# A combiner-attention and GeGLU kernel: keys kept as overlapping slices with the block maxima inside, values cast in the load, block means in column groups, and a new step order

## The chip, the cores and the metric

The kernel runs on one core of a Trainium2 chip. The metric is the device time of one execution in microseconds (us); "before" is 333.6 us (median of 3 runs, 333.51 to 334.36). Engines are named as in the profile: PE is TensorE, PEld its weight loads, DVE VectorE, ACT ScalarE, POOL GpSimd, SP SyncE. Transfers that change the type (fp32 in memory, bf16 on chip) are issued from POOL's queue; plain ones from the queues of SP and ACT. All executions used below were in the fast state (none lay more than 1.5% above the fastest of its kernel); medians are quoted.

## The reference, cut to what matters

```python
# attention: 4 batches, 8 heads, 768 positions, head size 64
k_sum = k.reshape(B, H, 24, 32, D).max(axis=3)       # maximum of each block of 32 keys
v_sum = v.reshape(B, H, 24, 32, D).mean(axis=3)      # mean of each block of 32 values
scores_l = scale * q @ k.T,   kept where |i - j| < 16          # the band
scores_s = scale * q @ k_sum.T + log(32)                       # 24 block scores
a = softmax(concat(scores_l, scores_s));  x = a @ concat(v, v_sum)
# GeGLU with a gated residual, 3072 tokens, 512 -> 1536 -> 512
out = x + sigmoid(x @ w_res) * ((gelu(x @ w_gate) * (x @ w_val)) @ w_out)
```

## The kernel before

The work is cut into 8 units u: half of a batch (384 positions). Each unit has a front part A of 12 FFN steps `fo` (gate and value products, Gelu, product `gvT`) and a back part B with the residual gate r, the down projection f and the output. The attention of unit u+1 is woven into part B of unit u; the loads, turns (transposes on PE) and block means of the next batch are woven into part A. In the profile tp are turns of K or Q, s the scores, P their exponentials under the mask, ao the attention output, xp its turns and xT their copy, g and vv the gate and value products, vs the block means, and th and o the last two operations of a unit's output.

In the attention, 64 queries of a head meet a window of 96 keys. The 128 rows of a score tile hold 96 band scores and, in rows 96 to 127, the block scores. Two products make them: one against a 128-wide slice of the turned keys, whose last 32 rows are garbage, then one that overwrites those rows:

```python
def k_step(b, hp, ...):                      # turn K of one head pair, then the block maxima
    transpose_pair(k_sb[b], kT[b % 2][hp], WIN, hp, pool, tag, copy)
    nc.vector.tensor_reduce(out=ksum[b % 2][hp][:, 0:NB], in_=kT..., op=ALU.max)

def s_step(u, hp, st):
    for t in range(HT):
        for hh in range(2):
            nc.tensor.matmul(s[:, hh, t*QT:(t+1)*QT], kt[ps, tt*QT:tt*QT+128], qt[...])
    for hh in range(2):
        nc.tensor.matmul(s[96:128, hh, 0:TU], ksum[b % 2][hp][ps, :], qt[...])   # block scores
    ...                                      # exp on ACT, mask product on DVE

def vsum_mm(b, pool, tag):                   # block means: 12 products into the same 32 rows
    for t in range(NT):
        nc.tensor.matmul(vs[96:128, :], bmat[:, t, :], vext[b % 2][0:BAND, t, :, 0:D], ...)
    nc.vector.tensor_copy(vsum[b % 2][96:128, :], vs[96:128, :])
# vsum_bc: the means are then copied by POOL behind each of the 12 value windows of vext
```

V of batch 0 comes as fp32 through the SP and ACT queues into a stage `vst` and is cast by 12 copies. K turns of the next batch stand in even units (after fo 1, 4, 7, 10), Q turns and the block means (after fo 6) in odd ones. [...]

The softmax here doesn't subtract the row's maximum and nothing guards it: scores larger than these inputs give would overflow.

Of the kernel before, what the change touches and what calls it, by code (L numbers as in the profile page):

```python
# [15 lines left out]
def kernel(  # L16
# [30 lines left out]
    KPAD = 832  # L47
# [6 lines left out]
    stage = ctx.enter_context(tc.tile_pool(name="stage", bufs=1))  # L54
# [12 lines left out]
    kT = [[const.tile([128, KPAD], BF16, name=f"kT{i}_{p}") for p in range(NP)] for i in range(2)]  # L67
    qT = [[const.tile([128, S], BF16, name=f"qT{i}_{p}") for p in range(NP)] for i in range(2)]
    ksum = [[const.tile([128, 32], BF16, name=f"ks{i}_{p}") for p in range(NP)] for i in range(2)]
    vext = [const.tile([128, NT, H, D + 1], BF16, name=f"vext{i}") for i in range(2)]  # L70
    vsum = [const.tile([128, DM], BF16, name=f"vsum{i}") for i in range(2)]
    w_gate = wpool.tile([128, KO, DFF], BF16, name="w_gate")
# [3 lines left out]
    vst = stage.tile([BAND, NT, H, D], F32, name="vst")  # L76
# [16 lines left out]

    k_sb, q_sb = {}, {}

    with tc.manual_schedule():

        k_sb[0] = load_qk(k, 0, 2, "k_sb")
        q_sb[0] = load_qk(q, 0, 2, "q_sb")
        nc.vector.memset(vst[0:32, 0], 0.0)  # L100
        nc.vector.memset(vst[64:96, NT - 1], 0.0)
        for t in range(NT):
            r0, r1, src = v_window(0, t)
            eng = nc.sync if t % 2 == 0 else nc.scalar
            eng.dma_start(out=vst[r0:r1, t], in_=src)  # L105


        nc.vector.memset(ident[:], 0.0)
        nc.gpsimd.affine_select(out=ident[:], in_=ident[:], compare_op=ALU.not_equal, fill=1.0,
                                base=0, pattern=[[-1, 128]], channel_multiplier=1)  # L110
        for i in range(2):
            for p in range(NP):
                nc.vector.memset(kT[i][p][:, 0:WIN], 0.0)
                nc.vector.memset(kT[i][p][:, WIN + S:KPAD], 0.0)
                nc.vector.memset(ksum[i][p][:], 0.0)
# [3 lines left out]
        nc.vector.memset(bmat[:], 1.0 / BLK)  # L119
        for i in range(2):  # L120
            nc.vector.memset(vext[i][:, :, :, D:D + 1], 1.0)
            nc.vector.memset(vext[i][0:32, 0, :, 0:D], 0.0)
            nc.vector.memset(vext[i][64:96, NT - 1, :, 0:D], 0.0)
        nc.gpsimd.affine_select(out=bias_t[96:128, :], in_=bias_t[96:128, :], compare_op=ALU.is_ge,
# [7 lines left out]
        nc.gpsimd.affine_select(out=bmat[:], in_=bmat[:], compare_op=ALU.is_ge, fill=0.0,  # L132
                                base=-WIN, pattern=[[QT, NT], [-BLK, 32]], channel_multiplier=1)
        nc.gpsimd.affine_select(out=bmat[:], in_=bmat[:], compare_op=ALU.is_ge, fill=0.0,
                                base=BLK - 1 + WIN, pattern=[[-QT, NT], [BLK, 32]], channel_multiplier=-1)
        nc.gpsimd.affine_select(out=bmat[:], in_=bmat[:], compare_op=ALU.is_ge, fill=0.0,
                                base=-WIN, pattern=[[0, NT], [0, 32]], channel_multiplier=1)
        nc.gpsimd.affine_select(out=bmat[:], in_=bmat[:], compare_op=ALU.is_ge, fill=0.0,
                                base=WIN + QT - 1, pattern=[[0, NT], [0, 32]], channel_multiplier=-1)
# [23 lines left out]
        def transpose_pair(src, dst, pad, hp, pool, tag, copy):  # L163
            tp = pool.tile([128, PJ, PP], BF16, tag=tag, name="tp")
            for j in range(PJ):
                for hh in range(2):
                    nc.tensor.transpose(tp[hh * 64:hh * 64 + 64, j, :], src[:, 2 * hp + hh, j, :],  # L167
                                        ident[0:PP, 0:PP])
            o = dst[:, pad:pad + S].rearrange("d (p j) -> d p j", j=PJ)
            t_in = tp.rearrange("d j p -> d p j")  # L170
            if copy == "act":
                nc.scalar.copy(o, t_in)
            else:
                nc.vector.tensor_copy(o, t_in)

        def k_step(b, hp, pool, tag, copy="act"):
            transpose_pair(k_sb[b], kT[b % 2][hp], WIN, hp, pool, tag, copy)
            nc.vector.tensor_reduce(
                out=ksum[b % 2][hp][:, 0:NB],
                in_=kT[b % 2][hp][:, WIN:WIN + S].rearrange("d (n w) -> d n w", w=BLK),  # L180
                axis=mybir.AxisListType.X, op=ALU.max)

        def q_step(b, hp, pool, tag, copy="act"):
            transpose_pair(q_sb[b], qT[b % 2][hp], 0, hp, pool, tag, copy)
# [7 lines left out]

        def vsum_bc(b, lo, hi, eng):
            src = vsum[b % 2][96:128, :].rearrange("p (h d) -> p h d", d=D)
            src = src.unsqueeze(1).to_broadcast([32, hi - lo, H, D])
            eng.tensor_copy(vext[b % 2][96:128, lo:hi, :, 0:D], src)  # L196

        def s_step(u, hp, st):
            b, half = u // 2, u % 2
            s = ps_s.tile([128, 2, 512], F32, tag="s", name="s")  # L200
            kt, qt = kT[b % 2][hp], qT[b % 2][hp]
            for t in range(HT):
                tt = half * HT + t
                for hh in range(2):
                    ps = slice(hh * 64, hh * 64 + 64)
                    nc.tensor.matmul(s[:, hh, t * QT:(t + 1) * QT], kt[ps, tt * QT:tt * QT + 128],  # L206
                                     qt[ps, tt * QT:(tt + 1) * QT], start=True, stop=True,
                                     skip_group_check=True)
            for hh in range(2):
                ps = slice(hh * 64, hh * 64 + 64)  # L210
                nc.tensor.matmul(s[96:128, hh, 0:TU], ksum[b % 2][hp][ps, :],  # L211
                                 qt[ps, half * TU:(half + 1) * TU], start=True, stop=True,
                                 skip_group_check=True)
# [23 lines left out]
        def xt_step(u, g, st, pool, tag):  # L237
            xp = pool.tile([128, 2, TU], BF16, tag=tag, name="xp")
            for i in range(2):
                ko = 2 * g + i  # L240
                for sub in range(NSUB):
                    nc.tensor.transpose(xp[:, i, sub * 128:(sub + 1) * 128],
                                        st["xn"][:, sub, ko * 128:(ko + 1) * 128], ident[:])
            nc.vector.tensor_copy(st["xT"][:, 2 * g:2 * g + 2, :], xp[:])  # L244
# [20 lines left out]
        def out_step(u, st, gvT, sub, part):  # L265
            ss = slice(sub * 128, (sub + 1) * 128)
            if part == 0:
                r = ps_mm.tile([128, 512], F32, tag="mm", name="r")
                for ko in range(KO):
                    nc.tensor.matmul(r[:], st["xT"][:, ko, ss], w_res[:, ko, :],  # L270
                                     start=(ko == 0), stop=(ko == KO - 1))
                th = work.tile([128, DM], F32, tag="th", name="th")
                nc.scalar.activation(th[:], r[:], AF.Tanh, scale=0.5)  # L273
                f = ps_mm.tile([128, 512], F32, tag="mm", name="f")
                for fo in range(4):
                    nc.tensor.matmul(f[:], gvT[:, fo, ss], w_out[:, fo, :],  # L276
                                     start=(fo == 0), stop=False)
                st["f"], st["th"] = f, th
            else:
                f, th = st["f"], st["th"]  # L280
                for fo in range(4, FO):
                    nc.tensor.matmul(f[:], gvT[:, fo, ss], w_out[:, fo, :],  # L282
                                     start=False, stop=(fo == FO - 1))
                nc.vector.scalar_tensor_tensor(th[:], th[:], 1.0, f[:], ALU.add, ALU.mult)  # L284
                o = work.tile([128, DM], F32, tag="o", name="o")
                nc.vector.scalar_tensor_tensor(o[:], th[:], 0.5, st["xn"][:, sub, :], ALU.mult, ALU.add)  # L286
                row = u * TU + sub * 128
                nc.sync.dma_start(out=out[row:row + 128, :], in_=o[:])

        def v_loads(b):  # L290
            for t in range(NT):
                r0, r1, src = v_window(b, t)
                nc.gpsimd.dma_start(out=vext[b % 2][r0:r1, t, :, 0:D], in_=src)  # L293


        for hp in range(NP):
            k_step(0, hp, ps_mm, "mm", "act")
            q_step(0, hp, ps_mm, "mm", "vec" if hp % 2 else "act")
        for t in range(NT):
            if t % 3 == 2:  # L300
                nc.scalar.copy(vext[0][0:BAND, t, :, 0:D], vst[:, t])
            else:
                nc.vector.tensor_copy(vext[0][0:BAND, t, :, 0:D], vst[:, t])
        st = new_unit()
        s_step(0, 0, st)
        s_step(0, 1, st)
        vsum_mm(0, ps_t, "t")
# [7 lines left out]
        xt_step(0, 0, st, ps_mm, "mm")  # L315
# [76 lines left out]
```

## Time and profile before

| stretch, before | us | how to read it |
|---|---|---|
| start to the first r of unit 0 | 71.8 | start of the first r product in the timeline |
| first r of unit u to first r of unit u+1 | 37.4, 34.6, 37.4, 34.6, 37.4, 32.3, 31.7 | part B of u and part A of u+1 |
| last first r to the end of the span | 15.2 | part B of unit 7 |

An interval from r to r is named here by its two units: 0 to 1, 2 to 3 and 4 to 5 hold the block means and Q turns; 1 to 2 and 3 to 4 hold K turns; the last two hold neither. The interval 6 to 7 also lacks the first score step of a next unit (21 instructions on ACT against 22 in 5 to 6, 249 products on PE against 263), which is why it is the shortest.

The list of waits of TensorE before (engine, tile and line, what it waited for: us in total, number of waits, longest):

```profile
PE tp L167 <- DMA k_sb<-in_k_dram: 13.9, 2, 9.3
PE g L255 <- DVE xT L244: 9.7, 7, 1.4
```

The timeline of the start before (start, us, engine, line, operation, output and inputs, shapes; in brackets the idle time in front and what ended it):

```profile
30.64 5.30 PE L189 MATMUL vs<-vext_113,bmat 96*32 96x512 bf16 x12
...
30.93 0.42 DVE L303 CAST vext_113<-vst 96x512 bf16<-96x512 f32 x1 [5.35 <-DMA vst<-in_v_dram]
...
46.45 1.38 PE L255 MATMUL g<-xT,w_gate 128*128 128x384 bf16 x4
...
54.41 0.85 PE L167 MATMUL tp<-ident,k_sb 96*64 96x96 bf16 x16 [4.64 <-DMA k_sb<-in_k_dram]
```

The fp32 V is complete only near 31 us, the block-mean product follows, and when the FFN has begun it stops: the K turns of batch 1 stand in unit 0's part A and wait 4.6 us for a load that has only come at 54.4 us.

Three intervals, r to r, in the windows view (busy us of each engine with the number of instructions, granted clock, DMA share, GB/s):

```profile
core 0: us, PE busy (x) PEld busy (x) DVE busy (x) ACT busy (x) POOL busy (x), PEclk, DMA share, GB/s
71.84:109.27 37.43, 35.99 (x339) 18.98 (x337) 17.53 (x34) 16.76 (x26) 7.43 (x6) 1.00 0.07 24
109.27:143.84 34.57, 33.14 (x327) 17.96 (x325) 19.92 (x37) 16.75 (x26) 8.71 (x12) 1.00 1.34 102
285.54:317.20 31.66, 30.23 (x249) 16.47 (x248) 16.22 (x32) 13.12 (x21) 0.00 (x0) 1.00 0.07 26
```

PE is busy about 96% of each, so from 72 us on only what shortens PE's own work, or removes PE's few waits, counts. The one regular wait is at the start of each unit:

```profile
158.03 0.50 PE L242 MATMUL xp<-ident,xn 128*128 128x128 bf16 x6
158.30 0.69 DVE L284 SCALAR_TENSOR_TENSOR th<-th,f 128x512 f32<-128x512 f32 x1 [0.91 <-PE f L282]
...
159.02 0.69 DVE L286 SCALAR_TENSOR_TENSOR o<-th,xn 128x512 f32<-128x512 f32 x1
159.63 0.55 DVE L244 COPY xT<-xp 128x768 bf16<-128x768 bf16 x1
160.23 0.48 PE L255 MATMUL g<-xT,w_gate 128*128 128x384 bf16 x2 [1.38 <-DVE xT L244]
```

The last turns of the attention output (xp) are on PE at 158.0, but their copy xT stands on DVE behind th and o of the old unit, and g waits 1.38 us for it.

### The profile page before, as it was taken

How to read it: one execution, taken by the hardware profiler on the slowest of the kernel's cores; microseconds unless marked ns; L12 is line 12 of the kernel's file. 1: busy time of each engine (PE TensorE's matmuls, PEld its weight loads, DVE VectorE, ACT ScalarE, POOL GpSimd, SP SyncE). 2: the span in 40 equal slices, each digit the busy share in tenths (PEclk: the TensorE clock that was granted, in tenths of full speed). 3: DMA queues.
4: the chain of work that ended last, by engine and by line, in shares of the span. 5: the costliest groups of instructions: out<-in, count | busy, mean ns of one | idle time of the engine just before them, and what ended most of it. 6: DMA issues, size and time to landing. Idle time of an engine off the chain costs nothing.

```text
span 332.4 us, 6258 instructions
## 1 busy us (share of the span) xinstructions
PE 284.7 (86%) x2640; PEld 153.8 (46%) x2640; DVE 162.4 (49%) x324; ACT 134.8 (41%) x202; POOL 71.1 (21%) x88
## 2 busy tenths in 40 slices
PE   0254574999899998999899989998999989998994
PEld 0241242554455445544445445544555446444641
DVE  5172651557533465556433665557333754474423
ACT  0343311464344543564336335553535523552320
POOL 7614741400007740000009440000042000000000
PEclk9999997999999999999999999999999999999999
DMA  8999999900100999001002997001000100010001
GB/s 155 206 197 192 202 207 178 92 3 35 65 0 3 159 154 113 1 2 63 34 0 26 198 151 52 1 34 40 26 2 0 65 34 0 2 63 34 0 33 63
DMA packets 54843, 23.95 MB, mean 72 GB/s; under 512 B 37408, under 2 KB 51744, under 8 KB 54816
## 3 DMA queue, kind: packets, MB, share of 16 engines
q0 software_dynamic: 42208, 14.98, 55.6%
q1 hardware_dynamic: 8032, 7.44, 8.0%
q10 hardware_dynamic: 4576, 1.15, 1.6%
q8 instruction: 20, 0.33, 0.4%
q14 instruction: 7, 0.06, 0.1%
HBM read 32.24 MB, written 6.29 MB: 116 GB/s over the span
## 4 chain that ended last, share of the span: by engine, by line
PE 75%; DMA 10%; DVE 9%; SPq 2%; issue 1%; POOL 1%; ACT 0%; DVEq 0%; ACTq 0%
PE g L255 19%; PE vv L259 19%; PE f L282 13%; DMA vst<-in_v_dram 6%; PE r L270 5%; PE f L276 5%; DMA k_sb<-in_k_dram 4%; PE vs L189 4%; PE tp L167 3%; DVE th L284 3%; DVE o L286 3%; PE ao L229 2%; PE s L206 2%; SPq L105 2%; PE s L211 2%
## 5 line engine op out<-in xcount | busy, mean ns | idle before, releaser
L255 PE MATMUL g<-xT,w_gate 128*128 128x384 bf16 x384 | 80.8, 330 | 9.7 <-DVE xT L244 9.7
L263 DVE TENSOR_TENSOR gvT<-ge,vv 128x384 bf16<-128x384 f32 x96 | 53.1, 553 | 73.2 <-PE vv L259 73.2
L262 ACT ACTIVATE ge<-g 128x384 f32<-128x384 f32 x96 | 47.1, 491 | 96.2 <-PE g L255 63.0
L259 PE MATMUL vv<-xT,w_val 128*128 128x384 bf16 x384 | 78.8, 328 | 0.0
L255 PEld LDWEIGHTS <-w_gate 128*128 128x128 bf16 x384 | 35.4, 99 | 34.9 <-issue 13.8
L259 PEld LDWEIGHTS <-w_val 128*128 128x128 bf16 x384 | 37.8, 98 | 25.5 <-issue 0.8
L215 ACT ACTIVATE P<-s,bias_t 128x768 bf16<-128x768 f32 x32 | 28.8, 901 | 46.0 <-PE s L211 45.9
L282 PE MATMUL f<-w_out,gvT 128*128 128x512 bf16 x192 | 45.4, 379 | 0.0
L196 POOL COPY vext_114<-vsum_116 32x2048 bf16<-32x2048 bf16 x6 | 11.1, 1893 | 86.7 <-DVE vsum_116 L191 86.7
L284 DVE SCALAR_TENSOR_TENSOR th<-th,f 128x512 f32<-128x512 f32 x24 | 16.5, 688 | 26.7 <-PE f L282 26.7
L282 PEld LDWEIGHTS <-gvT 128*128 128x128 bf16 x192 | 17.9, 98 | 20.6 <-issue 1.2
L218 DVE TENSOR_TENSOR P<-P,maskt 128x768 bf16<-128x768 bf16 x32 | 20.0, 626 | 14.5 <-ACT P L215 14.4
L270 PE MATMUL r<-w_res,xT 128*128 128x512 bf16 x96 | 24.9, 381 | 0.0
L276 PE MATMUL f<-w_out,gvT 128*128 128x512 bf16 x96 | 24.6, 379 | 0.0
L293 POOL DMA_DIRECT2D vext_114<-in_v_dram x24 | 18.2, 761 | 20.1 <-DMA q_sb<-in_q_dram 5.6
L167 PE MATMUL tp<-ident,k_sb 96*64 96x96 bf16 x256 | 10.1, 232 | 13.9 <-DMA k_sb<-in_k_dram 13.9
L196 POOL COPY vext_113<-vsum_115 32x2048 bf16<-32x2048 bf16 (+1 forms) x4 | 9.1, 2303 | 50.1 <-DVE vsum_115 L191 50.1
L235 DVE TENSOR_TENSOR xn<-ao,rz 128x384 bf16<-128x384 f32 x32 | 17.8, 558 | 1.1
L229 PEld LDWEIGHTS <-P 128*64 128x64 bf16 x384 | 9.2, 115 | 19.3 <-DVE P L218 10.1
L273 ACT ACTIVATE th<-r 128x512 f32<-128x512 f32 x24 | 14.3, 595 | 7.6 <-PE r L270 6.7
L286 DVE SCALAR_TENSOR_TENSOR o<-th,xn 128x512 f32<-128x512 f32 x24 | 16.6, 692 | 0.8
L167 PEld LDWEIGHTS <-k_sb 96*64 96x64 bf16 x256 | 7.9, 127 | 17.8 <-DMA k_sb<-in_k_dram 14.3
(139 smaller groups left out, 239.4 us busy)
## 6 DMA issues: line engine op xcount, KB each, us to landing
out_dram<-o SPq DMA_DIRECT2D x24, 256.0 KB, 2.0
k_sb<-in_k_dram POOLq DMA_DIRECT2D x3, 768.0 KB, 7.7
q_sb<-in_q_dram POOLq DMA_DIRECT2D x3, 768.0 KB, 11.3
vext_114<-in_v_dram POOLq DMA_DIRECT2D x20, 96.0 KB, 11.5
w_gate<-in_moe_w_gate_dram POOLq DMA_DIRECT2D x6, 256.0 KB, 16.1
w_val<-in_moe_w_val_dram POOLq DMA_DIRECT2D x6, 256.0 KB, 16.0
w_out<-in_moe_w_out_dram POOLq DMA_DIRECT2D x3, 512.0 KB, 14.0
vst<-in_v_dram ACTq DMA_DIRECT2D x5, 192.0 KB, 11.4
```

The lines of the kernel that those rows point to most:

```text
L167: nc.tensor.transpose(tp[hh * 64:hh * 64 + 64, j, :], src[:, 2 * hp + hh, j, :], ident[0:PP, 0:PP])
L196: eng.tensor_copy(vext[b % 2][96:128, lo:hi, :, 0:D], src)
L215: nc.scalar.activation(P.rearrange("p a t q -> p a (t q)"), s[:, :, 0:TU], AF.Exp, scale=scale, bias=bias_t[:])
L255: nc.tensor.matmul(g[:, 0:TU], w_gate[:, ko, fs], st["xT"][:, ko, :], start=(ko == 0), stop=(ko == KO - 1))
L259: nc.tensor.matmul(vv[:, 0:TU], w_val[:, ko, fs], st["xT"][:, ko, :], start=(ko == 0), stop=(ko == KO - 1))
L262: nc.scalar.activation(ge[:], g[:, 0:TU], AF.Gelu)
L263: nc.vector.tensor_mul(gvT[:, fo, :], ge[:], vv[:, 0:TU])
L270: nc.tensor.matmul(r[:], st["xT"][:, ko, ss], w_res[:, ko, :], start=(ko == 0), stop=(ko == KO - 1))
L276: nc.tensor.matmul(f[:], gvT[:, fo, ss], w_out[:, fo, :], start=(fo == 0), stop=False)
L282: nc.tensor.matmul(f[:], gvT[:, fo, ss], w_out[:, fo, :], start=False, stop=(fo == FO - 1))
L284: nc.vector.scalar_tensor_tensor(th[:], th[:], 1.0, f[:], ALU.add, ALU.mult)
L286: nc.vector.scalar_tensor_tensor(o[:], th[:], 0.5, st["xn"][:, sub, :], ALU.mult, ALU.add)
```

## The change

The intent: get rid of the second score product by writing the keys as 12 slices of 128 columns per head pair, 96 keys of a window with overlap plus 24 block maxima (copied into every slice); cast V of batch 0 in its load, as the other batches; run the block-mean products of batches 1 to 3 in four column groups of 32, side by side; warm PE up with 16 dummy products; put K turns, Q turns and block means one after another into odd units; copy xT in quarters instead of halves. The core of the diff:

```diff
-    kT = [[const.tile([128, KPAD], ...)]]; ksum = [[const.tile([128, 32], ...)]]
+    kW = [[const.tile([128, NT, 128], BF16, ...) for p in range(NP)] for i in range(2)]
-    vst = stage.tile([BAND, NT, H, D], F32, name="vst")          # and its 12 loads and 12 casts
+        v_loads(0)                                               # POOL queue, casts in the load
+            nc.vector.memset(vext[i][96:128, :, :, 0:D], 0.0)    # for i in 0, 1: before k_sb is loaded
@@ k_step
+            nc.scalar.copy(kw[:, 1:NT - 1, 0:BAND]..., src)      # 10 overlapping windows: 960 columns
+            nc.vector.tensor_copy(kw[:, 0, WIN:BAND]..., ...)    # the two edge windows
+            nc.vector.tensor_copy(kw[:, NT - 1, 0:BAND - WIN]..., ...)
+            nc.vector.tensor_reduce(out=ks..., op=ALU.max)
+            nc.vector.tensor_copy(kw[:, :, BAND:BAND + NB], ks.unsqueeze(1).to_broadcast([128, NT, NB]))
@@ s_step
-                nc.tensor.matmul(s[96:128, hh, 0:TU], ksum[b % 2][hp][ps, :], ...)
@@ block means of batches 1 to 3
+            for i in range(3):
+                for g in range(4):
+                    nc.tensor.matmul(vs[32 * g:32 * g + 32, :], bgrp[:, i, :], vext[...][0:BAND, 3 * g + i, :, 0:D],
+                                     ..., tile_position=(0, 32 * g))
+            nc.vector.tensor_copy(vpart[:], vs[:])
+            for g in range(4):
+                nc.sync.dma_start(out=vsum[b % 2][96 + 6 * g:102 + 6 * g, :], in_=vpart[32 * g:32 * g + 6, :])
@@ start
+        for i in range(16):
+            nc.tensor.matmul(wp[:], warm[:, 0:128], warm[:], start=True, stop=True)
@@ part A of odd units
+                    if fo < NP:          k_step(nb, fo, ps_t, "t")
+                    elif fo < 2 * NP:    q_step(nb, fo - NP, ps_t, "t")
+                    elif fo == 2 * NP:   vsum_grp(nb, ps_t, "t"); vsum_bc(nb, ...) x3 on POOL
@@ end of part B
+            end_step(u, st, 2)           # th, o
+            if nst:
+                xt_step(n, 2, nst, ps_t, "t"); xt_step(n, 3, nst, ps_mm, "mm")
 [...]
```

## The prediction

> **What bounds the kernel now.** (1) Start: in the timeline the first FFN matmul runs at 46.4 us, then TensorE stands from 49.8 to 54.4 us, because the K turns of batch 1 wait for their load (list of waits: tp on k_sb, 13.9 us in 2, the first 9.3). Before that the chain of waits runs through the fp32 V staging load (last casts at 27.8 and 30.9 us), the block-mean product (5.3 us) and the serial attention of unit 0. The r product of unit 0 stands at 71.9 us. (2) From there TensorE runs back to back (windows: busy about 96%): 245.5 us for seven units, then a 15 us tail. A plain unit takes 31.8-32.3 us, one with K turns 34.6, one with Q turns and block means 37.4.
>
> **Removed.** Block-score products: 0.27 us per head pair, 1.08 per unit. Part sits where VectorE sets the pace (th 0.70, o 0.69, reciprocal and xn 0.68, mask 0.5 between two f products), so I count 0.8: -5.6 us over seven units. Block means: 12 products of 512 columns, 2.73 us, become four 32-column groups side by side (Trainium skill, "TensorEngine Tiling (Array Packing)", When to Use Tiling; here 16 turns of 96 columns in 0.46 us already overlap): estimate 0.9 us, -5.5 us over three. The V stage and its 12 casts go. The K load of batch 1 is needed a unit later: the 4.6 us stall goes.
>
> **Added.** K copy of 960 instead of 768 elements on ACT (0.80 -> estimate 0.96 us); on VectorE two edge copies and a broadcast (estimate 0.6 us) per K step. K steps fall on four successive FFN steps: VectorE needs about 2.1 us per 1.86 us of PE, +0.8 us per odd unit. The block means go through four SyncE DMAs (0.33 us issue, 2 us landing) before three POOL copies of 1.9 us, with about 7.7 us until the values are wanted. These copies fall on the mask product and o; one mask took 2.9 instead of 0.56 us beside a POOL copy at 38 us (Trainium skill, "SBUF — State Buffer", Who interferes with whom: such a pair shares a locked port). I charge +2 us per odd unit. Otherwise the step order is nearly the old one: the 1.4 us wait of g for xT at a unit's start (9.7 us in all) stays, since o still precedes the last xT copies.
>
> **Start after.** Two memsets of 6144 elements (estimate 5.2 us each, from 0.485 per 512) hold VectorE to about 16 us; K steps end near 22; V lands about 21; weights are issued from 23 instead of 8.9 and finish near 51, just ahead of use; 16 warm-up products cost about 6 us. FFN starts near 40, r near 56.5 instead of 71.9.
>
> **Sum.** 56.5 + 4 x 31.4 + 3 x 39.7 + 15 = 316.2 of span, plus 1.2 = 317 us; range 308 to 325. Faster by over 2%: 0.92; within: 0.07; slower: 0.01.
>
> **Shows it right or wrong:** r of unit 0 at 52-61 us; no tp wait for batch 1's K; vs under 1.2 us; g still waiting 7 to 10 us for xT; ao waits behind vext copies of 1-3 us in units 1, 3, 5; plain units near 31.4.
>
> **What would break it:** weights late (FFN of unit 0 waiting on DMA), a longer chain of vsum DMAs and POOL copies, VectorE lag in K steps stalling turns, or the four column groups running one after another.

## The result and the profile after

After: 316.15 us (315.77 to 316.46, 4 runs) against 333.99 us for before in the same rounds; ratio 0.946, 95% interval 0.943 to 0.949. Ratios here are the mean time of one kernel's runs over that of the other's of the same rounds, so not quite the ratio of the medians. Run again beside the combinations at the end (c0), after took 317.43 us (315.44 to 317.65), 0.948 of before.

| stretch | before | after |
|---|---|---|
| start to first r of unit 0 | 71.8 | 56.7 |
| r to r, units 0 to 1, 2 to 3, 4 to 5 | 37.4 | 37.6 |
| r to r, units 1 to 2, 3 to 4 | 34.6 | 32.8 |
| r to r, units 5 to 6 | 32.3 | 32.9 |
| r to r, units 6 to 7 | 31.7 | 31.1 |
| tail | 15.2 | 15.3 |

15.1 of the 18.1 us of span saved lie before the first r; the seven intervals give 3.0 (245.4 to 242.3 us, sums of the table). TensorE's waits after:

```profile
PE g L269 <- DVE xT L258: 8.3, 7, 1.2
PE tp L167 <- DMA k_sb<-in_k_dram: 6.4, 1, 6.4
PE tp L167 <- DVE kW_0_88 L180: 3.6, 1, 3.6
...
PE ao L245 <- POOL vext_105 L217: 2.2, 2, 1.1
```

The second wait for K is gone (6.4 us in one, the first load). The wait of g for xT has stayed. New are waits of the turns for DVE and of the attention product ao for POOL. The start, in its timeline:

```profile
12.54 5.18 DVE L111 MEMSET vext_105<- 32x6144 bf16 x1 [1.34 <-issue]
...
19.35 0.19 DVE L178 COPY kW_0_88<-tp 128x80 bf16<-128x80 bf16 x1
...
23.55 5.54 PE L313 MATMUL wp<-warm 128*128 128x512 bf16 x15 [0.34 <-issue]
...
24.69 0.23 POOL L144 TENSOR_SCALAR_AFFINE_SELECT vext_104<-vext_104 32x8 bf16<-32x8 bf16 x1 [0.94 <-DMA vext_104<-in_v_dram]
...
25.46 0.78 POOL L154 DMA_DIRECT2D w_gate<-in_moe_w_gate_dram  x1
...
29.02 2.80 PE L197 MATMUL vs<-vext_104,bmat 96*32 96x512 bf16 x12
...
33.76 0.38 PE L245 MATMUL ao<-vext_104,P 128*64 128x65 bf16 x12 [1.65 <-DVE vext_104 L217]
...
35.17 0.55 PE L245 MATMUL ao<-vext_104,P 128*64 128x65 bf16 x12 [0.75 <-DVE xn L251]
...
39.95 1.49 PE L269 MATMUL g<-xT,w_gate 128*128 128x384 bf16 x4
```

Two memsets of 6144 elements (5.18 us each; the second is shown) hold DVE until 19.35 us, where the first K step can go on. V has landed at 24.69 us, when a POOL select that needs the last V window is let go, and only behind that select are the weights issued (25.46). The dummy products run from 23.55 to 29.0, the block-mean product follows at full rate. The first FFN product comes at 39.95 instead of 46.45, and nothing stops the FFN after it: from there to the first r it takes 16.8 instead of 25.4 us. So 6.5 of the 15.1 us are won before the FFN and 8.6 in its first part A: the wait of 4.6, about 2.3 of K turns, which moved into unit 1, and the rest of products at half rate behind the wait (granted clock 0.50 from 55 to 56 us in before). Note the two ao lines: 12 products take 0.38 us at 33.8, but 0.55 at 35.2. PE has slowed down again before the FFN begins.

Intervals 0 to 1, 1 to 2 and 6 to 7 in the windows view after:

```profile
56.71:94.32 37.61, 35.36 (x395) 19.02 (x393) 23.09 (x52) 20.18 (x30) 4.89 (x7) 1.00 1.08 84
94.32:127.13 32.81, 29.86 (x256) 16.44 (x253) 18.38 (x35) 13.74 (x22) 16.91 (x17) 1.00 1.53 108
267.92:299.05 31.13, 29.29 (x243) 16.20 (x241) 16.63 (x34) 13.37 (x21) 0.00 (x0) 1.00 0.07 26
```

DVE has more to do in the first (23.1 us instead of 17.5; K steps have moved into it), and POOL is busy 16.9 us of the second. What POOL does there shows in the timeline of unit 1's part B:

```profile
89.26 0.84 PE L205 MATMUL vs<-vext_105,bgrp 96*32 96x512 bf16 x12
...
90.95 2.93 SPq L211 DMA_DIRECT2D vsum_107<-vpart  x4
...
95.16 6.36 POOL L217 COPY vext_105<-vsum_107 24x2048 bf16<-24x2048 bf16 x3 [25.64 <-DMA vsum_107<-vpart]
...
96.23 1.23 DVE L234 TENSOR_TENSOR P<-P,maskt 128x768 bf16<-128x768 bf16 x1 [1.46 <-ACT P L231]
...
98.78 0.98 DVE L300 SCALAR_TENSOR_TENSOR o<-th,xn 128x512 f32<-128x512 f32 x1
99.28 0.25 PE L245 MATMUL ao<-vext_105,P 128*64 128x65 bf16 x4 [1.08 <-POOL vext_105 L217]
...
100.78 1.14 DVE L234 TENSOR_TENSOR P<-P,maskt 128x768 bf16<-128x768 bf16 x1 [0.33 <-ACT P L231]
```

The twelve block-mean products take 0.84 us (2.80 before), but their four pieces come back through four transfers, so POOL copies the means behind the value windows only from 95.2 to 101.5 us. ao waits 1.08 us for the second copy, and the mask products P (1.23 and 1.14 instead of 0.56 us) and o (0.98 instead of 0.69) are stretched beside the copies.

### The profile page after: what moved, and what is told of

The parts are those of the page before. It is cut to its first block, busy times and chain, and to the rows that moved or that the text cites. A ratio compares the mean times of both kernels' runs of the same rounds, so it can differ in the third digit from the quotient of the medians.

```text
span 314.3 us, 6217 instructions
## 1 busy us (share of the span) xinstructions
PE 271.4 (86%) x2569; PEld 149.3 (48%) x2592; DVE 180.2 (57%) x380; ACT 136.1 (43%) x200; POOL 82.5 (26%) x104
## 4 chain that ended last, share of the span: by engine, by line
PE 58%; DVE 27%; issue 5%; ACT 2%; POOL 2%; SPq 2%; DMA 2%; POOLq 1%; DVEq 0%; ACTq 0%
PE g L269 16%; PE vv L273 16%; PE f L293 13%; DVE th L298 4%; DVE o L300 4%; DVE ks L183 3%; DVE P L234 3%; PE ao L245 2%; DVE xn L251 2%; PE tp L167 2%; SPq L211 2%; PE r L283 2%; PE wp L313 2%; PE s L227 2%; DVE vext_105 L111 2%
## 5 line engine op out<-in xcount | busy, mean ns | idle before, releaser
L293 PE MATMUL f<-w_out,gvT 128*128 128x512 bf16 x274 | 65.3, 379 | 1.5 <-issue 1.1
L269 PEld LDWEIGHTS <-w_gate 128*128 128x128 bf16 x384 | 35.2, 98 | 32.8 <-issue 11.5
L273 PEld LDWEIGHTS <-w_val 128*128 128x128 bf16 x384 | 37.6, 98 | 25.9 <-issue 1.7
L293 PEld LDWEIGHTS <-gvT 128*128 128x128 bf16 x288 | 27.3, 98 | 31.0
L217 POOL COPY vext_105<-vsum_107 24x2048 bf16<-24x2048 bf16 x6 | 12.7, 2156 | 71.4 <-DMA vsum_107<-vpart 71.4
L298 DVE SCALAR_TENSOR_TENSOR th<-th,f 128x512 f32<-128x512 f32 x24 | 16.5, 688 | 23.1 <-PE f L293 23.1
L234 DVE TENSOR_TENSOR P<-P,maskt 128x768 bf16<-128x768 bf16 x32 | 21.4, 671 | 14.5 <-ACT P L231 14.5
L283 PE MATMUL r<-w_res,xT 128*128 128x512 bf16 x88 | 24.4, 381 | 0.4
L96 POOL DMA_DIRECT2D vext_105<-in_v_dram x24 | 18.2, 762 | 22.5 <-DMA w_out<-in_moe_w_out_dram 5.4
L96 POOL DMA_DIRECT2D vext_104<-in_v_dram x24 | 18.1, 762 | 13.0 <-DVE vext_104 L112 5.4
L217 POOL COPY vext_104<-vsum_106 24x2048 bf16<-24x2048 bf16 (+1 forms) x4 | 9.1, 2304 | 45.9 <-DMA vsum_106<-vpart 45.9
L251 DVE TENSOR_TENSOR xn<-ao,rz 128x384 bf16<-128x384 f32 x32 | 17.8, 558 | 1.1
L300 DVE SCALAR_TENSOR_TENSOR o<-th,xn 128x512 f32<-128x512 f32 x24 | 17.4, 727 | 0.8
L167 PE MATMUL tp<-ident,q_sb 96*64 96x96 bf16 x256 | 9.8, 226 | 7.6 <-DVE kW_0_88 L180 3.6
```

Of the source, the lines that this page charges most:

```text
L96: nc.gpsimd.dma_start(out=vext[b % 2][r0:r1, t, :, 0:D], in_=src)
L167: nc.tensor.transpose(tp[hh * 64:hh * 64 + 64, j, :], src[:, 2 * hp + hh, j, :], ident[0:PP, 0:PP])
L234: nc.vector.tensor_mul(Pf, Pf, maskt.unsqueeze(1).to_broadcast([128, 2 * HT, QT]))
L269: nc.tensor.matmul(g[:, 0:TU], w_gate[:, ko, fs], st["xT"][:, ko, :], start=(ko == 0), stop=(ko == KO - 1))
L273: nc.tensor.matmul(vv[:, 0:TU], w_val[:, ko, fs], st["xT"][:, ko, :], start=(ko == 0), stop=(ko == KO - 1))
L283: nc.tensor.matmul(r[:], st["xT"][:, ko, ss], w_res[:, ko, :], start=(ko == 0), stop=(ko == KO - 1))
```

## The experiments

The time came as predicted, so the experiments ask whether the terms of the sum did. Each kernel ran with 3 rounds, with runs of before beside them. Where a run is set against "after", 316.15 and 317.43 us (its two medians, from two sets of rounds) are the yardstick. In five profiles with an unedited start (after twice, a3, a4, b3) the first FFN product stood between 39.6 and 40.2 us and the first r of unit 0 between 56.2 and 58.1 us, so smaller differences at the start than these are not read; r-to-r intervals repeat to 0.1 us.

### b1 and b2: what part of the change made the start faster

b1 is the kernel before with one thing changed, K turns of the next batch in the odd unit:

```diff
-                    if half == 0:
-                        at(("A", 3 * hp + 1), lambda hp=hp: k_step(nb, hp, ps_t, "t"))
-                    else:
-                        at(("A", 3 * hp + 1), lambda hp=hp: q_step(nb, hp, ps_t, "t"))
+                    if half == 1:
+                        at(("A", hp), lambda hp=hp: k_step(nb, hp, ps_t, "t"))
+                        at(("A", NP + hp), lambda hp=hp: q_step(nb, hp, ps_t, "t"))
```

> Before, with only one thing changed: the K turns of the next batch stand in the odd unit (FFN steps 0 to 3, then Q in 4 to 7), as in the after kernel. Theory: the 4.6 us wait for batch 1's K load in unit 0 goes, and with it the half-rate matmuls that follow it (about 1.4 us): 6 us less, about 327.6 us. Rival: weights come late as well, so the wait only changes its name: under 3 us less.

Measured: 328.99 us (0.987 of before, interval 0.985 to 0.989; clear of noise), 4.3 us less, between the two. The wait for batch 1's K is gone and the first r comes at 62.0 instead of 71.8 us. But the odd intervals went from 37.4 to 40.5 us, 3.1 more, where the four moved turns cost 2.3 (the even intervals shrank by that much). The rest is one wait per odd unit that the list of waits has in b1 and not in before:

```profile
PE vs L189 <- ACT qT L172: 2.7, 3, 0.9
```

In b1 the block means stand in the same FFN step as a Q turn (after fo 6) and take the one buffer of the same pool, so they wait until ACT has copied Q out of it. That is what the expectation had left out. In after the means have a step of their own, and this wait is absent.

b2 is b1 with V of batch 0 cast in its load on the POOL queue; the stage and the 12 casts are gone:

```diff
-        for t in range(NT):
-            eng = nc.sync if t % 2 == 0 else nc.scalar
-            eng.dma_start(out=vst[r0:r1, t], in_=src)
+        for t in range(NT):
+            nc.gpsimd.dma_start(out=vext[0][r0:r1, t, :, 0:D], in_=src)     # behind K and Q
-                nc.vector.tensor_copy(vext[0][0:BAND, t, :, 0:D], vst[:, t])  # or nc.scalar.copy
```

> The kernel b1, and V of batch 0 also cast in its load on the POOL queue instead of the fp32 stage and 12 casts. Theory: K, Q and V no longer share the DMA engines with each other's stage, V is complete near 22 us, the first FFN product comes near 36 instead of 46.4 us: 9 to 10 us less than b1, about 318 us. So the start gives nearly the whole gain of the change, and the slices, column groups and new order together only about 2 us net. Rival: the weights, issued from 22 us instead of 9, hold the FFN of unit 0: 2 to 5 us less than b1.

Measured: 320.36 us (319.82 to 322.63, 6 runs), 8.6 us less than b1. In the profiled execution (322.63 us, the longest of the six) the first FFN product stands at 35.2 us, but unit 0's f products then wait 2.05 us for w_out and go on at half rate (four take 1.86 instead of 1.02 us), and the first interval is 44.2 instead of 40.5 us. So the theory holds for V, and the rival names the next limit. b2 does not separate the cast from the order, though: with V ahead of them on POOL's queue, the weights are issued from 25.4 instead of 8.9 us, so V (landed at 24.6) no longer moves while they do. Which of the two brought V in sooner was not tested. These two steps alone bring 12.9 us of the 16.8 to 17.8 that the whole change brings. They still carry the three waits of vs (2.7 us), which neither before nor after has; without these they would bring about 15.6 us (an estimate), so that the slices, column groups, warm-up and order are worth only 1 to 2 us together.

### a1: without the warm-up products

```diff
-        wp = ps_mm.tile([128, 512], F32, tag="mm", name="wp")
-        for i in range(16):
-            nc.tensor.matmul(wp[:], warm[:, 0:128], warm[:], start=True, stop=True)
```

> After, without the 16 warm-up products. Theory: the start won its time through the loads, not through the warm-up; the 16 products stand on the chain of waits for 5.5 us and win back 2.5 us of the block-mean product (2.8 instead of 5.3 us), so without them the first FFN product comes near 37 us instead of 39.9 and the whole kernel takes about 313.3 us, 2 to 3 us less. Rival: the warm-up is what makes the start fast (matmuls at half the rate cost more than it): 1 to 4 us slower than the after kernel.

Measured: 314.00 us (313.71 to 314.46), 2.2 to 3.4 us less than after; first r at 54.5 us. The theory holds: the dummy products cost more than they save. The Trainium skill, "TensorE: Matmul & The Clock Gate", Part 1, says that PE runs at half rate until it has been busy for about 3.4 us, and falls back when idle for as long. The trace of after agrees with the first: the block-mean product took 2.80 instead of 5.30 us behind the warm-up. The second came sooner here: the windows view gives a granted clock of 1.00 up to 34.6 us and 0.50 from 34.7 to 40 us, though PE had not been idle for more than 1.65 us at a time since the warm-up (it was busy 0.77 of the 2.7 us before the fall). The warmth was gone before the FFN, the only place with enough work to repay it. One trap: before its first recorded change the view shows 1.00, also where a1's block-mean product takes 5.30 us, so at the start go by how long the products take.

### b4: zeros off VectorE's path

```diff
-            nc.vector.memset(vext[i][96:128, :, :, 0:D], 0.0)          # both buffers, ahead of everything
+        nc.vector.memset(vext[0][96:128, :, :, 0:D], 0.0)              # after the small zeros; V's strips first
+        nc.gpsimd.memset(vext[1][96:128, :, :, 0:D], 0.0)              # on POOL, behind the weights' issues
```

> After, with the zeros of the mean rows of the second V buffer written by POOL after the weights' issues, and those of the first after the small zeros (V's strips first). Theory: VectorE is free near 9 us instead of 19.3, V is issued from 4.5 instead of 9.9 us and complete near 21 instead of 24.7, the block-mean product ends near 25-26 instead of 31.9: 5 to 7 us less, about 310 us. Rival: loads alone set the start (K and Q, then V, then weights): 2 us less or nothing.

Measured: 312.88 us, 3.3 to 4.6 us less than after: short of the theory, above the rival. DVE was free for the K steps at 12.6 instead of 19.35 us, and V was issued from 4.5 instead of 9.9 us, but it landed no sooner:

```profile
12.59 0.24 DVE L178 COPY kW<-tp 128x80 bf16<-128x80 bf16 x1
12.74 1.69 POOL L96 DMA_DIRECT2D vext<-in_v_dram  x2 [1.63 <-DMA q_sb<-in_q_dram]
...
24.40 0.23 POOL L144 TENSOR_SCALAR_AFFINE_SELECT vext<-vext 32x8 bf16<-32x8 bf16 x1 [1.50 <-DMA vext<-in_v_dram]
...
25.21 2.80 PE L197 MATMUL vs<-vext,bmat 96*32 96x512 bf16 x12
...
36.00 1.49 PE L269 MATMUL g<-xT,w_gate 128*128 128x384 bf16 x4
```

V lands at 24.4 us in b4 and at 24.7 in after: it comes behind Q in any case (at 12.74 us its issue waits for Q), and it moves slowly (windows view of after: 205 GB/s from 5 to 10 us with K and Q, 111 from 15 to 20 with V). V's pieces are 256 bytes of fp32 per row and head; the Trainium skill, "DMA: Bandwidth & Descriptors", Specifications, gives 512 bytes as the least for full rate, which this agrees with, though no run here changed the size. So the memsets had been one limit of the start and V's landing is the next, 3 to 4 us behind it. The prediction took V to land at 21.

### a2: the block-score products put back

```diff
+            for hh in range(2):
+                nc.tensor.matmul(s[96:128, hh, 0:TU], kw[ps, 0, BAND:128], qt[ps, half * TU:(half + 1) * TU], ...)
```

> After, with the two block-score products per head pair put back beside the slices (they write the same values again, 0.27 us of TensorE each pair). Theory: about 0.7 us per unit come back over seven units and 0.5 us in the start, 5 to 5.5 us more, about 321.5 us, because in two of the stretches between f products VectorE's th, o, reciprocal, xn, mask set the pace. Rival 1: all 1.08 us of each unit lie on the path: 8 us more, 324 us. Rival 2: the products were hidden: under 2 us more.

Measured: 322.23 us (321.41 to 322.73), 6.1 us more than after's median in its first rounds, 4.8 more than in the second. The intervals say where: 38.26 instead of 37.61 in odd, 33.2 instead of 32.8 in the next, 31.51 instead of 31.13 in the last, so 0.65 x 3 + 0.39 x 3 + 0.38 = 3.5 us in seven units (0.4 to 0.65 of the 1.08 us removed per unit). In the start the first FFN product comes at 40.86 us, 0.7 to 1.3 us later than in the five profiles; the first r at 58.8 us is 2.1 us later than in after's first profile but only 0.7 later than in its second, where PE stayed at half rate as long as here (until 44.3 us; 41.5 in the first), so more than about 1 us is not shown for the start. The theory holds in kind, since the product is partly hidden behind DVE's chain, and the prediction's 0.8 us per unit was too high.

### a3: xT ahead of th and o

```diff
-            end_step(u, st, 2)
             if nst:
                 xt_step(n, 2, nst, ps_t, "t")
                 xt_step(n, 3, nst, ps_mm, "mm")
+            end_step(u, st, 2)
```

> After, with the last two xT copies of a unit put ahead of th and o of the last sub-tile on VectorE. Theory: the wait of g for xT (8.3 us in 7 waits) is the time of th and o in front of the copies, so it falls to about 0.3 us each and the kernel to about 310 us, 6 to 7 us less. Rival: the wait is the hand-over from the turns to the copies and back, or f's buffer held longer takes it back: under 2 us less.

Measured: 307.71 us (307.1 to 307.89; 0.920 of before), 8.4 to 9.7 us less than after. Every interval is 1.2 us shorter (36.4, 31.6 and 29.9). The wait is not only shorter but gone, as the same place in unit 2 shows for after and for a3:

```profile
140.88 0.50 PE L256 MATMUL xp<-ident,xn 128*128 128x128 bf16 x6
141.15 0.69 DVE L298 SCALAR_TENSOR_TENSOR th<-th,f 128x512 f32<-128x512 f32 x1 [0.94 <-PE f L293]
...
141.87 0.69 DVE L300 SCALAR_TENSOR_TENSOR o<-th,xn 128x512 f32<-128x512 f32 x1
142.48 0.61 DVE L258 COPY xT<-xp 128x384 bf16<-128x384 bf16 x2
142.89 0.59 PE L269 MATMUL g<-xT,w_gate 128*128 128x384 bf16 x2 [1.18 <-DVE xT L258]
```

```profile
138.66 0.50 PE L256 MATMUL xp<-ident,xn 128*128 128x128 bf16 x6
...
139.00 1.03 PE L269 MATMUL g<-xT,w_gate 128*128 128x384 bf16 x4
139.03 0.62 DVE L258 COPY xT<-xp 128x384 bf16<-128x384 bf16 x2 [1.04 <-PE xp L256]
...
139.57 0.68 DVE L298 SCALAR_TENSOR_TENSOR th<-th,f 128x512 f32<-128x512 f32 x1
...
140.28 0.69 DVE L300 SCALAR_TENSOR_TENSOR o<-th,xn 128x512 f32<-128x512 f32 x1
```

In a3 the copies run at once and g's four products go through without a bracket. th and o come later, and TensorE's list of waits names neither.

### a4 and b3: what the column groups are worth

a4 moves the block means from FFN step 8 to step 4; b3 leaves them at 8 but makes them by twelve products in a row:

```diff
a4:  -  k: fo 0-3, q: fo 4-7, vsum_grp: fo 8       +  k: fo 0-3, vsum_grp: fo 4, q: fo 5-8
b3:  -  vsum_grp(nb, ps_t, "t")                    +  vsum_mm(nb, ps_t, "t")
```

> After, with the block means of the next batch after FFN step 4 instead of 8 (the Q turns move back by one step). Theory: units 2, 4 and 6 begin late because unit 1, 3 and 5's attention waits for the POOL copies of the means, and its mask and o products are slowed beside them; with the copies over 7 us earlier r to r after an odd unit falls from 32.8 to 31.1-31.4 us, 4 to 5 us less in all, about 311.5 us. Rival: that difference has another cause (K and Q turns shifted, loads): less than 1.5 us.

> After, with the block means of batches 1 to 3 by the twelve products one after another (2.73 us instead of 0.8), written straight to their rows, without the four SyncE DMAs. Theory: TensorE pays 1.9 us more per odd unit, but the POOL copies start 2.3 us earlier and the wait for them (about 1.7 us) goes: 0 to 2 us slower in all. Rival: the column groups are worth their TensorE time: 5.7 us slower, 322 us.

Measured, a4: 313.10 us (312.91 to 313.24), 3.1 to 4.3 us less than after (theory 4 to 5). Intervals 1 to 2, 3 to 4 and 5 to 6 are 31.50 instead of 32.8 us, 1.3 each; the odd ones did not change (37.65). The waits of ao for POOL are gone, and P at the same place takes 0.56 again. The interval after the means is what the theory said (31.1 to 31.5), so the POOL copies were its cause. That a4 also moved the Q turns does not matter: b3 leaves them where they were and gives the same 31.5.

Measured, b3: 317.54 us, 0.1 to 1.4 us more than after, inside the theory's 0 to 2. The odd intervals rise to 39.58 (+1.97, PE's time for the longer product), the next fall to 31.51 (-1.30, the wait gone, since the means skip the four transfers). Each batch thus gained 0.67 us from the column groups as they were placed, a third of what PE saved; with the copies out of the way (a4) it keeps all of it. The Trainium skill, "TensorEngine Tiling (Array Packing)", When to Use Tiling, gives four-fold column tiling for a product with 32 weight columns, and the trace agrees in kind (2.80 to 0.84 us for twelve of 512 columns, 3.3 times). That each tile writes partitions of its own the page says too, but not what it costs to bring the results together again.

### c0 to c3: the edits together

> The after kernel itself, unedited, beside the combinations: 316.2 us as before, to 0.5 us. It is the yardstick for how far the start alone moves from run to run (first r of unit 0 stood at 56.2 to 57.2 us in four kernels whose start is the same).

> After with three edits at once: xT ahead of th and o, block means after FFN step 4, zeros off VectorE's path; warm-up kept. Theory: they act in different stretches and add up, 8.4 + 3.1 + 3.3 us less than 316.2: about 301.4 us. Rival: the start is now held by w_out's landing (b4's r to r of unit 0 was already 0.95 us longer), so the start's part is lost again: 304 us or more.

> After with four edits at once: xT ahead of th and o, block means after FFN step 4, zeros off VectorE's path, no warm-up. Theory: in b4 TensorE waited for V to land (24.4 us) anyway and the warm-up filled that wait, so without it the block-mean product runs at half rate (5.3 instead of 2.8 us) after V has landed: 1 to 2.5 us slower than the combination with warm-up, about 303 us. Rival: the warm-up costs what a1 showed in any kernel: 2 us faster than with it, about 299.5 us.

> c2 and one edit more: the POOL selects on the last V window and the second V buffer stand after the weights' issues, so the first weights are issued without waiting for V to land (22.7 instead of 25.2 us) and the DMA engines have no gap. Theory: V's landing still sets the block-mean product, so only unit 0's wait for w_out goes: 0.5 to 2 us less than c2. Rival: the weights now share the DMA engines with V's last windows and V lands later: no gain or a loss.

c2 is a3 + a4 + b4; c1 leaves out the warm-up as well; c3 is c2 with the POOL selects that are not needed at once put behind the weights' issues:

```diff
+        nc.gpsimd.affine_select(vext[0][0:32, 0, :, D:D+1] ...)      # only this one ahead of the weights
         nc.gpsimd.dma_start(out=w_gate..., w_val..., w_res..., w_out...)
+        nc.gpsimd.affine_select(...)                                 # the other three behind them
```

| kernel | median us (range) | ratio to before (95%) | first r of unit 0 | interval 0 to 1 |
|---|---|---|---|---|
| c0, after again | 317.43 (315.44 to 317.65) | 0.948 (0.944 to 0.951) | 58.1 | 37.6 |
| c1, all, no warm-up | 301.21 (300.84 to 302.07) | 0.902 (0.900 to 0.903) | 51.9 | 38.0 |
| c2, all, warm-up | 300.71 (300.44 to 301.06) | 0.900 (0.898 to 0.901) | 52.9 | 37.3 |
| c3, weights sooner | 299.62 (298.98 to 300.31) | 0.896 (0.894 to 0.898) | 52.1 | 36.4 |

c0 took 1.3 us more than expected. Its profile shows it in the start, where PE stayed at half rate until 44.3 us instead of 41.5 (windows view), and its first r is 1.4 us later, with the same intervals behind it. c2 is where the sum of the single gains had put it (expected 301.4). In c1 TensorE waits 2.2 us for V and then runs the block-mean product at half rate (5.30 us, from 21.4 us on), but that product begins so much earlier that the first FFN product still comes 1.0 us before c2's (35.0 against 36.0). The first interval takes 0.7 us of this back (the f products wait 1.4 us for w_out in c1, 0.7 in c2). The medians are 0.5 us apart with overlapping ranges, and the profiled executions 0.2 us the other way, so no difference between c1 and c2 is shown: neither the theory's 1 to 2.5 us nor the rival's gain of 2. So the warm-up costs 2 to 3 us where TensorE would otherwise work (a1), and nothing that these runs can show where TensorE waits for V and then for w_out. In c3 the first weights are issued at 22.9 instead of 25.1 us, no wait for w_out is left, and it is 1.1 us below c2, as expected, and the fastest kernel: 299.6 us, 0.896 of before.

## Why the prediction was right, and where its terms were not

The total was right (317 predicted, 316.15 measured), and so was the main reason: the start. Point by point:

- **First r near 56.5 us.** 56.7 measured, FFN from 39.95 (predicted 40). The parts were less exact, and that they met the sum is in part luck: DVE was held to 19.35 us, not 16 (2.7 us of this is issue time, 1.3 in front of each big memset); K steps ended at 25.75, not 22; V landed at 24.7, not 21; the weights were issued from 25.5, not 23, and w_out landed near 54 to 56 us (an estimate: its issues took 13.4 to 15.3 us to land, the last went out at 40.7), not 51. It did not show because the warm-up ran to 29.1 us over the K steps and V's landing, and no f product had to wait for w_out. (The 5.2 us per big memset were right, but 0.485 us per 512 elements would give 5.8; the memsets of 96 and 384 elements, 0.14 and 0.38 us, give 5.2.) b1 and b2 confirm the two causes named: the K load needed a unit later (4.3 us in all, an estimated 7 without the three waits of vs) and V's stage, cast and order taken together (8.6 us).
- **Block scores, -5.6 us over seven units.** The mis-sized term: a2 gives 3.5 in the units, 0.5 each instead of 0.8, and 0.7 to 1.3 before the FFN, which the prediction did not list.
- **Block means, 0.9 us instead of 2.73.** 0.77 to the next product in the timeline, so 1.97 us of PE saved. Right in size.
- **POOL copies, +2 us per odd unit, with waits of 1 to 3.** a4 gives 1.3; the waits of ao in after are 1.08 us. Right in cause, a third too large. The Trainium skill, "SBUF — State Buffer", Who interferes with whom, says that a VectorE instruction with two inputs in SBUF contends with a GpSimd instruction that reads SBUF. The trace agrees: the two stretched mask products ended at 97.46 and 101.92 us, 0.4 us behind the end of the POOL copy beside each (97.05 and 101.52). The prediction also booked it to the wrong interval: part B of an odd unit lies in the interval behind it. Hence "39.7 and plain 31.4" became 37.6, 32.8 and 31.1; without the copies in it (a4, b3) a plain interval takes 31.5. The sums are near (244.7 predicted, 242.3 measured).
- **K steps, +0.8 us per odd unit.** FFN steps with K take about 2.04 us, with Q 1.87 (timeline of unit 3, from 144.05 to 152.21 and 154.07 to 155.94), so 0.7 for four. Right.
- **The wait for xT stays, 7 to 10 us.** 8.3 us; a3 shows that its cause is the one named.
- **Warm-up about 6 us.** 5.5 us on the chain of waits; net cost 2.2 to 3.4 us (a1).

Left open: how much of V's earlier landing is due to the cast in the load and how much to the weights going out behind it; and why V's transfer takes some 12 us (from 12.7 to 24.4 in b4), of which no run changed the shape.

## What to carry to other kernels

In a start that waits for loads, ask first which load is needed when, and in which order they share the queue: moving one consumer by a unit, and casting V in a load that goes out ahead of the weights, gave three quarters of this change as measured. When a step is moved, look for a new neighbour that shares its buffer: b1 lost 0.9 us per odd unit to that. An operation that TensorE waits for should not be issued on its engine behind one that nobody waits for: swapping two lines (a3) gave 8.4 us or more. Before splitting a product over column groups, follow its result to its last reader and place it early enough that the extra hops are hidden.

## What the Trainium skill lacked or had wrong

- "TensorEngine Tiling (Array Packing)", Performance Considerations: it names PSUM evacuation as the cost after tiling, but not the way back across partitions. Here four column groups saved 1.97 us of PE per batch and their four transfers and late copies took back 1.30 (b3).
- "TensorE: Matmul & The Clock Gate", Part 1: it tells how PE warms up, but not when dummy products pay. Here 16 of them cost 2.2 to 3.4 us where PE had work (a1) and made no difference that shows where it waited for loads (c1 against c2). Its table puts the fall to half rate after an idle window of about 3.4 us; in after the clock fell at 34.7 us with no idle time over 1.65 us since the warm-up (12 ao products took 0.38 us at 33.8, 0.55 at 35.2).
- "VectorE: DVE Perf Modes", Zero memsets can be issued as uint32: it counts one cycle per element for a memset, which at the page's 0.96 GHz gives an estimate of 6.4 us for 6144 elements; the trace shows 5.18 us, 0.84 ns per element.
